# A searched instruction order, searched further from its present state: a new table for four attention layers

## The chip, the cores and the metric

The kernel runs on one core of one Trainium2 chip. The metric is device microseconds (us) of one execution; lower is better. Five engines run their own instruction streams side by side: TensorE (PE, with its weight loads shown as PEld), VectorE (DVE), ScalarE (ACT), GpSimd (POOL) and SyncE (SP, which only issues DMAs here). Each takes its instructions strictly in the order in which they were written.

## The reference

Four layers on a sequence of 2048 tokens by 512 features: A, B, A, B. Layers 1 and 3 are the same linear attention block, layers 2 and 4 the same sliding-window block.

```python
def _A_ref(x, wqkv, wo):               # linear attention, 32 heads of 16
    q, k, v = heads(x @ wqkv)
    phi = lambda t: where(t > 0, t + 1, exp(t)) + 1e-6
    pq, pk = phi(q), phi(k)
    kv = einsum("bhsd,bhse->bhde", pk, v);  z = pk.sum(over tokens)
    return merge((pq @ kv) / (pq . z + 1e-6)) @ wo

def _B_ref(x, wqkv, wo):               # softmax over a causal window of 256
    q, k, v = heads(x @ wqkv)
    p = softmax(where(0 <= i - j < 256, q @ k.T * Dh ** -0.5, -1e9))
    return merge(p @ v) @ wo

x = x + _A_ref(_layernorm(x), A_wqkv, A_wo)
x = x + _B_ref(_layernorm(x), B_wqkv, B_wo)
x = x + _A_ref(_layernorm(x), A_wqkv, A_wo)
x = x + _B_ref(_layernorm(x), B_wqkv, B_wo)
```

## The kernel before

The 2048 tokens are 16 tiles of 128 (T = 16). Everything stays in SBUF between the layers: the residual `xres`, the transposed activations or queries `XQ`, the keys `kB`, the values `vB` and three or four tiles of probabilities (`pb`, and in the last layer also the upper part of `vp`). PSUM's eight banks are each one tile of 512 float32 columns.

A class `Plan` writes the whole program as a list of 2542 small operations with their dependences; nothing is emitted yet. The operations, with the lines that the profile shows:

- The layer norm (`norm`): statistics on DVE (L382, L383), the power of -1/2 on POOL (L384), the normalised tile on DVE (L385), and its transposition by a DMA that SP issues (L391) or, for a few tiles, by PE (L397).
- Products of a tile with a weight matrix: L420 (tokens on partitions: 4 matmuls of 512 columns) and L434 (features on partitions: 16 matmuls of 128 columns). ACT or DVE copies the result out of PSUM (L409; L615 and L616 for the sliding-window keys; L404 for tiles transposed by PE).
- Linear attention: the feature map phi by an exponential on ACT (L443) and DVE or ACT steps (L444, L447, L448, L450); sums over tokens (L476, L479, L501, L524); denominators (L563), their reciprocals (L567, L568), spreading (L576) and scaling of the queries (L583).
- Sliding window: for every tile of keys, four score groups and a "far" group (L667; L709 and L712 for the far one), each into four PSUM banks; two exponentials per group on ACT (L677, L722) that read two banks each; the masks of the window's edges on DVE (L687, L736, L745) or POOL (L686, L733, L744), where either engine may do it; the values (L768, L780); the reciprocal and the division (L790, L791) on DVE; the output product (L420) and the residual (L594).
- SP issues the DMAs: loads of inputs (L291) and weights, the transpositions (L391), the rearrangement of keys and values into `kB` and `vB` (L624, L643), and most of the stores (L891; POOL issues the others).

What sets the order: a constant `TABLE` (L903 on), text that is unpacked in `place`. For every operation it holds its position in one global order, the engine that runs it (where more than one may), the PSUM bank of every tile, and which of its waits comes first. `place` adds the dependences that follow from two tiles sharing a bank, and lets a long POOL operation wait for the last wide DVE operation ahead of it. `synchronise` turns dependences into semaphore waits and leaves out those that are already implied. `Kernel.run` then lets each engine play its operations in the table's order:

```python
order = [ops[raw[2 * k] + 256 * raw[2 * k + 1]] for k in range(n)]
o.eng = ("PE", "ACT", "DVE", "POOL", "SP")[raw[2 * n + o.i]]
x.banks = [raw[3 * n + k]]
o.first = raw[3 * n + len(tiles) + o.i]
```

So one table decides who waits for whom. The score group that PE issues next needs four free banks, and those come free when ACT has read them; the other PSUM tiles come free when ACT or DVE has copied them out.

Of the kernel before, what the change touches and what calls it, by code (L numbers as in the profile page):

```python
# [231 lines left out]
class Plan:  # L232
# [675 lines left out]
    r"g^ch*omMqeSyc&Ms#I#As-h}G6&S1-PN}L84yvlQs=cbFLMQ{TR5^7^-BFp~p88S!png)Jlt48I4-w$5N(c@HsYFl&GJ}PP5E&vtJJmr2g2eDz{j7$lkSe^&",
    r"0)Zh4G*C$)v`PY5AsMuTqL3YmL3Jn&*&qj$gy5<MlvGh6In;!lPz!=UZ72bCpp+`F8mdxITNPEsR5VBdxu6WxgJ#ei+CxVu4RxUjEK|LpDYSr=&<et+Sx`sy",
    r"hUKa?Ojc7=akWCNQd3n2*r_@}7w7{K)JoM2cB$2Bx|*iCLTBg;Jz$3F2WM1w=n4JdteOMo)Iiv+_NoC;Q_Y1HP+zTt%`gx4!G5@)R>6FDqZU9twFQDgBefc4",  # L910
    r"!$MdC;nX7dMV(iRVUG$1OW?j*3+v#bs;jm_SoN!_rG8iI;R;-ZYj6PesRwEs41&S19S*`{cmjuDDLhn<)DC#8mcbC%2}9v2jD#C-7?#6zc%p8?GYAeFU>IzK",
    r"TQD3p!4U`n3IT7!E?`8w10liSQ8)>Nr(gsKeh<&#G`xV9up5G6aNGmIa4)=qd+-DNrYzot`w$YN!vpvZT48Gpg(0vFI*b8lAT&n7NEjL4sz7)QjzeJl1=?a5",
    r"j0q<o2>uFDu@L?UvEVm|4bd<rM#orK7>i&|%!M&9CFaI_SO8ODJ3I^du^0BnqL><sVF?@s8qYy)cnIgA59WbK@DmirpCKj0#)8-n^TKE-g{3hK=7aq38cJdu",
    r"EQ4|J0;GaBkQ(}9JdBSCa3EI30azBR;_r|K(qc7Ch*hvUriDZ}9MfTYtc4@7HrBwJco8l^ddz}hF)NP1u6P;3VK#gV-7qh9$MDz}2V-KagB?)QZj69KF%L2s",
    r"8Ur116pqF{I0Wm%SZn}wF$oUB9Jm+9U^yIz4WSX#!=zXNJ7H&xh~=>{Ou=MW9}nOmJc!e<3ns^@m;$HcFg$`Y@Gw@wnV11*<2LMxvv3X`!|ga0Cc;t7h?y`u",
    r"R>b4D15e;S90#j$4Q9rZI05G3c<6ywaV@UH^|%2W;3?dQr|}G)#cS9QU*S0{3+3QE{(wK?ehf<GAvkTq>v#i$Q3a?7H}MvRr4SUJ?qE22i?>nHU3Byl{)}k}",
    r"C>=Gz^z<6%;e1?xjnUFQ3{2y35(J_NI1wYzPV7jNu@g;(khB?tP-hBFTW}KQr3;vkLeW-?M$zda=BF^U3ol_YDozXWGA_c!_y%K8Oo~MrC?hq&*i?vwN>C<>",
    r"OYx{MUBNgskOt8bEJgQmFcqN(_z;_7Gb~A^sT`G|qEwceV++hdIjJS)q6$=i9$|c{PBmy4m8Y6iiykA=2pUBdX(<k;+Vl%%rYZ0QyHGtELkTD$)uH-Smqrs&",
    r"B8o_n=~qllN$4qdrQfg*jiZ7TiN;f3`W=r_7D`GD=ok&9Ni>0yQ8$W0{b(63$K#Zhrcig9Oi^hhJ;PIUhO$vZYDBZ?G>xUHG>6X73T#Z@VRmXl6R9c9rIok}",
    r"zsC!7facM8szlFmJ~gA}^a2l39(sw3XaOyz<dmB#(?U8#DX0piq)Rk}QqfuJK|QGj^`g`?fUeMGN<$%aZ<-1h=_*Z!84yZ`*4GI1b*f6!;07(BnSgpLO(W9V",  # L920
    r"=mb@xrL>Gr(h-_L+vz4vrybOvZqahuNh|0!X}yc?(0zJ9dG#!cq$BGnI;zg6TT&~^uXocPT1i240UcBa)8TY$T15{jf^I|MbwvG$+R|fsM&Hp)il(FM82Sm7",
    r")vTXVIUP$IJy6Hdv2|P>Ru9tUbxeJj2J5?&RIjE=I<ZcotLS7pxlW-g>y)~huCDh|DxF%3uA%QyO+8Uh()Dy0y^pHu$-05AufL~)`Z?{VLOQs9LA7)mZS_lf",
    r"ML$ppT~e3QwRLm-BZbgwXqv90Tj;d9u1=@Z>*>0J9;3(V8G4rfiJZ=$1L<)(qYkVa>e)J;o})AA%sPQ?seh(cy0xyThv@ivk)EkH(Gp!ox6^BBsBWVd>-Kt>",
    r"UPqg$ux_i@(-vx^H&7FON>A0Lbq9S~C(^HJxZX%_sIg9{=jo<;fnKeDr}=uRE~3xqx71P3)ob(=y-=UmN_Wz~(66*suhS#+Z*)<2)>-rgy<T6|SM(-bR2S15",
    r"^hSMEU(=g)7u{6{=G*$N4#LItNPR~K<q3L}Zl=5G(fYc+q`T`I`lvppZ|Ylmyw0k#=_mS}4#C-VC=SV6^gVrC=g>LzQ@vGh)6evFy+ePe!*Dnb%irtgIy>j!",
    r"m->Z%r6aK69$GjeN8+<OC%5Lv9GsWwHr!J$*Zs8RUV5hv#{KmQ9ff=AA9OC=mXGlXeVn850DV&T(W`V{eP8F+CpaqS(Ld_Y{FDA!hvx@62Jg}jbzI)9V{$x>",
    r"&L{b`4#Wl6aV##xr}!zK=9T)fzQoV?G8g3UI1k6?eEdf5(cg1kPQVHIIVa)5{EL3UN%;yV;v$@z6LULiPcOL`AJWM<7k8i%oS%QyMfnw1<l=l-|G;~7DgKd<",
    r"=#u<M@6)Auzy3{E;sd%1$Kivz8&~EkT$Q_W4X()@xEfdIT6~^6a&qp(DL5sk;y&Du`|<_u&KJ2er{*;LyY9hhxhKEX1DIIzK<>}&xfjpl1$>6j@_g>igLp8<",
    r"<{^BJnTN9CVVsW3aBT)I%fq=2kKnpojw^6I{*~+VNN&Il`8U4Gv-leS&eyp-&*9m8gKzR%zQxOU1>a`mJ3N=~@^W6pOIVr3ypr$nQohflcp;DGcKm=F@hTp}",
    r"Yj`!U<*~eu*K-!m${TqD|HPYk9B1RryoJZ}1pb-R^F*$1w(>U4z}`!R+0L(d2WR9ryptRAF8+m^@NUk;nZ1W(3vS8U?BT$sDF-o=crx#0Hm%s0pk^O8<6veA",  # L930
    r"H!%BoIydLw<^YSC%G3BT&)_3$jWaX(ARpz2e24>?NBo$da5fXx<TqJOPLti_GI>n_liL(Dg-kw^!xT1oOmtJkgfK--L(|BFG;K{d)7bPh#Y__u%Cs}R%uqAT",
    r"G&P}3d(+G`Hyun1)7x}3oy>64$8<K~O<xnn#4wReWYf<?FfGk&Gsny|txOlw)wDLNOdHeR3^2t_L^HyaFj35Wv)YU_3(P>X#w;{ZO-!@jEHWicDHF{cFx^Z!",
    r")7=a*gH0JT&y+Qb&02HN#4<h15mVYMHOowFGsGM<$INoG-W)fh%xJU0Y%~+hCUe4^G!xAQGs%2sCYvc{iJ5A?H|xxEbIFV`(@Y$5(Zn^U%w`i`;+fOtjJayI",
    r"nD}O_Nnl=>aVCKz6fNmxyh$X7jVG-fG8ts6S!s5e73QqjZ8AzSbJ?6X=gc*e+}t#K%oS7Kh@>#n%`LOd>@^ikO7qrOQR3vbxnn@?ntLXMyfK+1r2Jw+$pdrW",
    r"q%t$iLla15n!xhXyfQ%~v;1m)FbPd)nJ<Y<VzWT@nOP>R{APm6LJ2MrC6XjDi6x0-Fd0o`2_wNIizGFf%ytt_c9^V^*<_QQ=0_7nqDmGML$XUWi7u%mhdeSr",
    r"nbZ<fa!ML0AU~Ue(p*Sho5$vcNh;S(E_q^FNFhOKBu~xnrlk~?Jd#`5NGvHLZKbiqmb}tL+DTD~BPAuS<d=L>OiD;8DK2THw6vFwQbx*34=E=Vq`Xv=iYA$K",
    r"kV>Yf^pf6E*))~pl0rI36;oYmNL7<kx=1srX2wfRX)Rr)vviYMGC?NFaXBF;Wx33f+EPclOKMX|`pQa~EvICKERi(ky7ZA7vQ%2hB$+IyC7sNX2(nD($p)z`",
    r"b>*g<k+eo^I+NZ^5o?{DD*dFMY?M{9N!CaesVb|by166MWT4!YK~lramBF%B&dLzECz~a_43%MWPKL{R86hKOoqR8&<hi_%`qDry$$i->m!+X>kx(|Y-6;>`",
    r"iaeC<@<?_`Ap2N$%N}_m*CdP$Y_~}e`&7P@y|PaV+0k-U_R9e|D9>b!M6uEASlJ<k?R1H17t11vZj0C%@`Ie0{_>;5w72DugtZssmc+0%O?Vr@&Xl0`m0Xkr",
# [176 lines left out]
```

## Time and profile before

| | |
|---|---|
| median of 3 runs | 409.51 us (408.73 to 409.90) |
| the profiled execution | 408.54 us, of which the instructions span 406.7 us |
| busy: PE, ACT, DVE, POOL | 383.5, 355.2, 317.7, 163.7 us |
| granted TensorE clock | 0.999 |

The span is what the trace shows from the first instruction to the last; 1.8 us of the execution's time lie outside it. The span falls into six stretches that the prediction uses: 0 to 60 us the first linear layer with the loads; 60 to 210 the sliding-window layer 2, into which the first parts of layer 3 are already mixed; 210 to 260 the turn through layer 3 to layer 4; 260 to 398 layer 4; and the last tile until 406.7.

### The profile page before, as it was taken

To read this page: it belongs to the slowest core of one execution; us is meant where nothing else is said; L and a number is where in the kernel's file an instruction comes from. 1 tells how busy PE (TensorE), PEld (TensorE's weight loads), DVE (VectorE), ACT (ScalarE), POOL (GpSimd) and SP (SyncE) were. 2 spreads that over 40 slices of the span, in tenths; PEclk is the share of its full clock that TensorE was granted. 3 is DMA by queue.
4 is the path that set the end of the run, shared out by engine and by line. 5 is a ranking of instruction groups with operands and counts; after the bars stand their busy time and mean duration, and the time that the engine had idled before them with its cause. 6 is when DMAs were issued, how large, how long until landed. Compare 5 with 4: busy or idle time off the path is not lost.

```text
span 406.7 us, 18121 instructions
## 1 busy us (share of the span) xinstructions
PE 383.5 (94%) x7920; PEld 257.3 (63%) x7995; DVE 317.7 (78%) x715; ACT 355.2 (87%) x464; POOL 163.7 (40%) x261
## 2 busy tenths in 40 slices
PE   8999999999989999999999999999899999989886
PEld 4554777667556556575657767677658665756664
DVE  6985899978998898887684799986796759665455
ACT  4976999999999999999997365898999899999991
POOL 4563132424454454341545202044451346323872
PEclk9999999999999999999999999999999999999999
DMA  7777125442437524434232000434314442473451
GB/s 228 142 174 193 31 67 114 102 94 72 91 69 138 79 77 96 113 84 91 56 69 56 15 2 27 121 84 107 75 50 99 92 121 57 112 136 93 97 135 54
DMA packets 67286, 37.75 MB, mean 93 GB/s; under 512 B 47880, under 2 KB 62344, under 8 KB 67208
## 3 DMA queue, kind: packets, MB, share of 16 engines
q1 hardware_dynamic: 66816, 35.54, 38.4%
q8 instruction: 63, 1.03, 1.0%
q0 software_dynamic: 384, 1.05, 0.7%
q14 instruction: 15, 0.12, 0.1%
q10 hardware_dynamic: 8, 0.00, 0.0%
HBM read 6.29 MB, written 2.10 MB: 21 GB/s over the span
## 4 chain that ended last, share of the span: by engine, by line
PE 59%; ACT 26%; DVE 7%; issue 3%; DMA 3%; POOL 1%; SPq 1%; POOLq 0%
PE ps L420 21%; PE ps L434 15%; ACT pb L677 14%; PE ps L768 8%; PE ps L667 6%; ACT pb L722 4%; ACT vp L677 4%; PE ps L780 3%; PE ps L501 2%; ACT tE L443 1%; DVE stats L382 1%; DMA XQ<-vp 1%; PE ps L712 1%; DMA xres<-in_A_x_dram 1%; DVE xres L594 1%
## 5 line engine op out<-in xcount | busy, mean ns | idle before, releaser
L677 ACT ACTIVATE pb<-ps 128x1024 bf16<-128x1024 f32 (+3 forms) x224 | 197.9, 977 | 8.0 <-PE ps L667 7.1
L384 POOL TENSOR_TENSOR rs<-mv,negh 128x1 f32<-128x1 f32 x64 | 38.2, 596 | 89.6 <-DVE mv L383 87.2
L434 PE MATMUL ps<-xT,wBp 128*128 128x128 bf16 x1024 | 68.9, 219 | 1.3 <-DVE o L791 0.3
L434 PEld LDWEIGHTS ps<-xT,wBp 128*128 128x128 bf16 x1024 | 58.6, 98 | 12.7 <-issue 4.1
L768 PEld LDWEIGHTS ps<-vB,pb 128*128 128x128 bf16 x1712 | 54.0, 96 | 11.6 <-issue 3.6
L768 PE MATMUL ps<-vB,pb 128*128 128x52 bf16 (+1 forms) x1712 | 59.7, 184 | 0.5 <-POOL vp L744 0.2
L744 POOL TENSOR_SCALAR_AFFINE_SELECT pb<-pb 128x1024 bf16<-128x1024 bf16 x36 | 42.0, 1167 | 41.6 <-DVE xn L385 11.8
L667 PE MATMUL ps<-XQ,kB 32*128 32x256 bf16 (+2 forms) x1024 | 48.3, 262 | 3.0 <-ACT pb L677 0.9
L722 ACT ACTIVATE pb<-ps 128x1024 bf16<-128x1024 f32 x50 | 48.4, 1029 | 3.2 <-PE ps L712 2.3
L594 DVE TENSOR_TENSOR xres<-ps,xres 128x512 bf16<-128x512 f32 x63 | 43.0, 685 | 10.3 <-PE ps L420 9.8
L686 POOL TENSOR_SCALAR_AFFINE_SELECT pb<-pb 128x512 bf16<-128x512 bf16 x46 | 30.6, 666 | 46.4 <-ACT pb L677 25.0
L420 PE MATMUL ps<-wA,XQ 128*128 128x512 bf16 x176 | 46.6, 379 | 2.1 <-issue 0.6
L443 ACT ACTIVATE tE<-ps 128x512 bf16<-128x512 f32 x64 | 38.2, 609 | 10.1 <-PE ps L420 3.6
L382 DVE BATCH_NORM_STATS2 stats<-xres 128x6 f32<-128x512 bf16 x64 | 43.3, 682 | 2.7 <-DMA xres<-in_A_x_dram 2.2
L790 DVE RECIPROCAL rc<-ps 128x16 f32<-128x16 f32 x64 | 14.0, 238 | 30.3 <-PE ps L780 30.2
L434 PE MATMUL ps<-XQ,wA 128*128 128x128 bf16 x512 | 35.7, 219 | 0.0
L434 PEld LDWEIGHTS ps<-XQ,wA 128*128 128x128 bf16 x512 | 30.9, 98 | 6.8 <-issue 0.6
L667 PEld LDWEIGHTS ps<-XQ,kB 32*128 32x128 bf16 x1024 | 15.4, 92 | 29.0 <-ACT pb L677 11.3
L420 PE MATMUL ps<-wBv,xT 128*128 128x512 bf16 x102 | 28.9, 380 | 4.3 <-issue 1.8
L420 PE MATMUL ps<-wBo,oT 128*128 128x512 bf16 x108 | 29.6, 380 | 2.8 <-issue 1.4
L420 PE MATMUL ps<-M,XQ 128*128 128x512 bf16 x115 | 30.1, 380 | 1.7 <-issue 0.6
L733 POOL TENSOR_SCALAR_AFFINE_SELECT pb<-pb 128x256 bf16<-128x256 bf16 x50 | 22.2, 467 | 19.7 <-DVE pb L745 4.1
(128 smaller groups left out, 602.6 us busy)
## 6 DMA issues: line engine op xcount, KB each, us to landing
vB<-vS SPq DMA_DIRECT2D x64, 136.0 KB, 2.6
kB<-vp SPq DMA_DIRECT2D x64, 128.0 KB, 2.2
xres<-in_A_x_dram SPq DMA_DIRECT2D x6, 256.0 KB, 4.6
wA<-in_A_wqkv_dram SPq DMA_DIRECT2D x4, 256.0 KB, 3.5
pb<-in_B_wqkv_dram SPq DMA_DIRECT2D x4, 256.0 KB, 3.2
out_dram<-xres POOLq DMA_DIRECT2D x8, 128.0 KB, 3.1
out_dram<-xres SPq DMA_DIRECT2D x7, 128.0 KB, 2.4
xres<-in_A_x_dram SPq DMA_DIRECT2D x4, 128.0 KB, 2.2
```

The costliest lines, as they stand in the source:

```text
L382: self.on("DVE", "stats", lambda e: e.bn_stats(K.stats[:, t % 8, 0:6], K.xres[:, t, :]), key, dve(512), rd=[("xres", t)], wr=[("stats", t ...
L384: self.pow = self.on("POOL", "pow", lambda e: e.tensor_tensor(K.rs[:, t, :], K.mv[:, t, 1:2], K.negh[:], ALU.pow), key + 0.03, (640, 690), ...
L420: m = e.matmul(K.ps(ps), lhs(c), rhs(c), start=c == 0, stop=c == 3)
L434: m = e.matmul(K.ps(ps)[:, f * P:(f + 1) * P], w(c, f), xT(c), start=c == 0, stop=c == 3)
L443: self.on("ACT", "E", lambda e: e.activation(K.tE[:, s, :], K.ps(ps), ACT.Exp, bias=0.0), key, act(512), wr=[("tE", s)], ps=[ps])
L594: self.on("DVE", "res", lambda e: e.tensor_tensor(K.xres[:, t, :], K.ps(po), K.xres[:, t, :], ALU.add), key, dve(512), rd=[("xres", t)], w ...
L667: m = e.matmul(K.ps(two(gq // 2)[gq % 2])[:, ns * i:ns * i + ns], K.kB[rows, j % 4, 2 * f + b, :, :], K.XQ[rows, f, q:q + ns], start=True, ...
L677: return e.activation(out(h, ns).rearrange("p (f g) c -> p f g c", f=n), i, ACT.Exp, bias=0.0, scale=0.25)
L686: return e.affine_select(out=x, in_=x, compare_op=ALU.is_ge, fill=0.0, base=1, pattern=[[0, 4 * n], [2, 64]], channel_multiplier=-1)
L722: return e.activation(o.rearrange("p (f g) b c -> p f g b c", g=2), i, ACT.Exp, bias=0.0, scale=0.25)
L744: return e.affine_select(out=x, in_=x, compare_op=ALU.is_ge, fill=0.0, base=-2, pattern=[[0, 16], [-2, 64]], channel_multiplier=1)
L768: m = e.matmul(K.ps(ps[f // 2])[:, cols(f, gq, wide(f, gq))], stat(b, f, gq)[:, c:c + P], vals(b, f, gq, wide(f, gq)), start=f % 2 == 0 an ...
```

## The change

The order is searched further from its present state, with 48 draws a move and a higher first temperature. In the program that means a new `TABLE` and nothing else: the same 2542 operations, the same dependences, another global order, for some operations another of their allowed engines, and other PSUM banks. The core of the diff, one line of some sixty:

```diff
 TABLE = (
-    r"c-p;L1E3yBv+b(t>gtYd+qP}nwr$(CZQHhO+q=OcS>(;!{QF*#O?H#){%`L0&2;y4pE`A_x@PXZ5mh7=RXuj7@~dbHlv0sZ0aZ|?R%ujPRY*lwqDU21=@hFN",
...
+    r"c-qBT1HdK6(k->twr$(CZQHhO+qP}nw(VdyStPsr&+M1v1-nUhllT7lzB|*?Q&oNH)ajm?dkG>#REP%op#VH~2oWI?q=qz55DGzBC=5jaAUZs8k6a0e0S2l-",
...
 )
```

What moves, counted over the engines' streams (before to after). ACT has 463 operations before and 458 after: the weight rearrangements of L374 go from 5 to 2, the fills of L361 from 1 to 0 and of L863 from 3 to 2, the copies after a transposition (L404) from 12 to 10, the copies of L409 from 32 to 33, the key copies of L615 from 6 to 7. All 256 and 56 exponentials of L677 and L722 stay. DVE has 714 and 723: the long masks of L745 go from 16 to 22, those of L687 from 24 to 25 and of L736 from 23 to 25, L404 from 1 to 3, L409 from 62 to 61, L616 from 26 to 25. POOL has 224 and 219: the long masks of L744 go from 40 to 34, L686 from 48 to 47, L733 from 66 to 62, while L374 goes from 3 to 6, L359 from 1 to 2 and L861 from 1 to 2. PE has the same 896 operations.

PE's stream differs mostly in three regions: its first 60 us, the end of layer 2 with the turn (about 165 to 275 us), and single neighbours exchanged in between. The order of the 156 score groups is the same throughout. The PSUM banks are numbered anew almost everywhere; which operation frees a bank for which is often the same under the new numbers.

SP at the program's start (the loads of `xres` tiles and of `wA`, and the transpositions of normalised tiles into `XQ`), before:

```order
L294 DMA wA<-in_A_wqkv_dram 128x4x512
L291 DMA xres<-in_A_x_dram 128x2x512 x2
L391 DMA_TRANSPOSE XQ<-vp 128x4x128
L291 DMA xres<-in_A_x_dram 128x2x512
L391 DMA_TRANSPOSE XQ<-vp 128x4x128 x2
L291 DMA xres<-in_A_x_dram 128x2x512
L391 DMA_TRANSPOSE XQ<-vp 128x4x128
```

and now:

```order
L294 DMA wA<-in_A_wqkv_dram 128x4x512
L291 DMA xres<-in_A_x_dram 128x2x512
L391 DMA_TRANSPOSE XQ<-vp 128x4x128
L291 DMA xres<-in_A_x_dram 128x2x512 x2
L391 DMA_TRANSPOSE XQ<-vp 128x4x128
L291 DMA xres<-in_A_x_dram 128x2x512
L391 DMA_TRANSPOSE XQ<-vp 128x4x128 x3
```

The first transposition has moved ahead of one load, and two loads now stand between the first and the second. Both streams have the same loads; the first two normalised tiles that are transposed by DMA are tiles 5 and 7 before, 5 and 6 now.

ACT at the turn, from the last four score groups' exponentials of layer 2 (L722 and L677) into the feature maps of layer 3 (L443), with `oT` the transposed output of layer 2's last tile, before:

```order
L443 ACTIVATE tE<-ps 128x512
L677 ACTIVATE pb<-ps 128x4x128 x2
L677 ACTIVATE pb<-ps 128x4x64 x2
L677 ACTIVATE pb<-ps 128x4x128 x2
L404 ACTIVATE oT<-ps 128x512
L443 ACTIVATE tE<-ps 128x512 x4
L404 ACTIVATE XQ<-ps 128x4x128
L409 ACTIVATE vp<-ps 128x512
```

and now:

```order
L443 ACTIVATE tE<-ps 128x512
L677 ACTIVATE pb<-ps 128x4x128 x2
L677 ACTIVATE pb<-ps 128x4x64 x2
L677 ACTIVATE pb<-ps 128x4x128 x2
L863 ACTIVATE vp<-zc 128x1152
L443 ACTIVATE tE<-ps 128x512
L409 ACTIVATE vp<-ps 128x512
L443 ACTIVATE tE<-ps 128x512 x7
```

The copies of `oT` and of one transposed tile of `XQ` have left ACT for DVE, and a fill of `vp` has come from POOL and stands where the copy of `oT` stood.

ACT in layer 4, around tiles 5 to 7 of the keys (about 300 to 323 us), with L615 the copy of new keys and L409 that of queries or values, before:

```order
L722 ACTIVATE pb<-ps 128x8x2x64 x2
L677 ACTIVATE pb<-ps 128x4x224 x6
L722 ACTIVATE pb<-ps 128x8x2x64 x2
L677 ACTIVATE pb<-ps 128x4x224 x10
L409 ACTIVATE XQ<-ps 128x4x128
L722 ACTIVATE pb<-ps 128x8x2x64 x2
```

and now:

```order
L722 ACTIVATE pb<-ps 128x8x2x64 x2
L677 ACTIVATE pb<-ps 128x4x224 x6
L722 ACTIVATE pb<-ps 128x8x2x64 x2
L615 ACTIVATE vp<-ps 128x512
L677 ACTIVATE pb<-ps 128x4x224 x8
L409 ACTIVATE XQ<-ps 128x4x128
L677 ACTIVATE pb<-ps 128x4x224 x2
L722 ACTIVATE pb<-ps 128x8x2x64 x2
```

One copy of keys has come from DVE to ACT and stands between the exponentials; the copy of queries has moved two exponentials forward.

More of the change, by code (lines that the diff above doesn't have):

```diff
@@ L908 @@
[L908 to L939, printed above, removed]
@@ L960 @@
+    r"{E+NVD~~O&y7WQs9~5SMA$oz?Pu8ah{k;#wXTpO696*cDpZ{LqPZ?h+LIJ^jqX04a=U_ZWe3+h{rv+abp4>gYKIqs>)zhPY)r06^LecOg8~#Zjetr~$e}n@6",
+    r"3G9Eg;h*>5M=U<-^4|o8Uzk3AK`HSc*YMXz{G9UPZy|ro{}09aXukL<@4uVQ&q(kK1cbi@L;r$oKfu9%VPgLiDgIKKe_iQcG7<hlh+jNU@E<Q9|BWT-zdPRl",
+    r"PnLgCieCzX|1{E{CV(Hmhv8>3f}ckt{x9jrFVPkLyG6y%%?-a`7T{kyehJn11@}h$IQ#ggqx|MeoKI@^{{YyWG8z",
 )
```

75 lines of the change are left out of this document (52 added, 23 removed).

## The prediction

> **What bounds the kernel now.** I read the page's busy times first, then the busy times of the six stretches, then who waits for whom on PE, and last the timeline at single waits. The page's first part says how full the engines are:
>
> ```profile
> span 406.7 us, 18121 instructions
> PE 383.5 (94%) x7920; PEld 257.3 (63%) x7995; DVE 317.7 (78%) x715; ACT 355.2 (87%) x464; POOL 163.7 (40%) x261
> ```
>
> PE is idle for 406.7 - 383.5 = 23.2 us in all, and no order of the same instructions can take more than that from it. The busy times by stretch (after the times: length, then PE, PEld, DVE, ACT, POOL) show where:
>
> ```profile
> 7.00:60.00 53.00, 52.12 (x556) 32.69 (x563) 44.30 (x119) 44.17 (x78) 22.38 (x42) 1.00 0.56 136
> 60.00:90.00 30.00, 29.40 (x513) 20.01 (x518) 25.72 (x59) 28.77 (x35) 9.52 (x14) 1.00 0.48 101
> 90.00:210.00 120.00, 114.07 (x2469) 73.68 (x2491) 101.35 (x220) 116.50 (x134) 52.32 (x67) 1.00 0.40 86
> 210.00:260.00 50.00, 48.37 (x827) 34.92 (x834) 40.01 (x89) 31.23 (x54) 12.13 (x17) 1.00 0.16 37
> 260.00:330.00 70.00, 66.84 (x1693) 48.16 (x1704) 53.34 (x113) 65.43 (x82) 28.74 (x51) 1.00 0.38 90
> 330.00:398.00 68.00, 62.02 (x1768) 42.20 (x1776) 44.18 (x98) 66.55 (x84) 33.75 (x56) 1.00 0.46 105
> ```
>
> Two kinds of stretch alternate. From 7 to 60 and from 210 to 260 us PE is the bound: it idles 0.9 and 1.6 us there, and ACT has 8.8 and 18.8 us to spare. From 90 to 210 and from 330 to 398 ACT is: it idles 3.5 and 1.5 us, and PE waits for it. From 60 to 90 and 260 to 330 both are nearly full (ACT idles 1.2 and 4.6 us, PE 0.6 and 3.2). So the room for a better order is what the bounding engine idles in each stretch: 0.9 + 1.2 + 3.5 + 1.6 + 4.6 + 1.5 = 13.3 us, 3.3% of the time; the rest of PE's idle time is the price of ACT's work. Some of PE's idle time is no order's business either: from the list of waits on PE,
>
> ```profile
> PE ps L420 <- issue: 4.5, 28, 0.2
> PE ps L1029 <- DVE kB L1021: 1.3, 1, 1.3
> PE ps L420 <- ACT pb L677: 1.2, 2, 0.7
> PE ps L420 <- DVE rc L790: 1.1, 3, 0.5
> PE ps L667 <- ACT pb L677: 0.9, 3, 0.5
> PE ps L420 <- DMA XQ<-vp: 0.2, 1, 0.2
> ```
>
> 4.5 us in 28 pieces have no releaser ("issue"), 1.3 us are the start. The others are many and short. What they look like, PE at two places of layers 2 and 4:
>
> ```profile
> 113.14 0.40 PE L667 MATMUL ps<-XQ,kB 32*128 32x256 bf16 x8
> 114.27 0.81 PE L420 MATMUL ps<-wBv,xT 128*128 128x512 bf16 x3 [0.73 <-ACT pb L677]
> 115.52 0.40 PE L667 MATMUL ps<-XQ,kB 32*128 32x256 bf16 x8 [0.44 <-DVE o L791]
> ...
> 372.73 0.62 PE L434 MATMUL ps<-xT,wBp 128*128 128x128 bf16 x8 [0.32 <-DVE o L791]
> 373.66 0.71 PE L712 MATMUL ps<-XQ,kB 32*64 32x64 bf16 x64 [0.31 <-ACT pb L677]
> ```
>
> Each is a PSUM bank that ACT or DVE has not yet emptied.
>
> **The change part by part.** PE's work, the exponentials and the order of the 156 score groups stay. I went through the 39 places where PE lost most (the step from one operation's end to the next against the quick quarter of the same pairs) and asked which operation frees the bank or brings the data there in the new table. At 35 of them it is the same operation as before, under another bank number, among them the waits at 114.27, 115.52 and 373.66 above; at 372.73 the bank now comes from an exponential. Those waits I cost at nothing: they stay. That leaves five edits.
>
> The start. PE waits there for one transposition by DMA:
>
> ```profile
> 17.75 1.90 PE L420 MATMUL ps<-wA,XQ 128*128 128x512 bf16 x8 [0.24 <-DMA XQ<-vp]
> ```
>
> The new order issues the first transposition ahead of a load, transposes tile 6 second, and asks for tile 7 later on PE, so these 0.24 us can go; the loads that now stand behind the transpositions bring the tiles from 10 on, which PE's stream takes well after tile 7. The stretch holds 0.9 us in all. Bounds: a gain of 0.9, a loss of as much if a load comes late. I take a gain of 0.2. What is late next is PE itself, which is then gap-free up to 60 us.
>
> ACT in the first 60 us loses three weight rearrangements and two fills:
>
> ```profile
> L374 ACT ACTIVATE wBp<-pb 128x512 bf16<-128x512 bf16 x5 | 3.7, 767 | 0.0
> L863 ACT ACTIVATE vp<-zc 128x1152 bf16<-128x1152 bf16 x3 | 3.5, 1154 | 0.0
> ```
>
> 3 x 0.77 + 2 x 1.15 (the second kind of fill priced like the first) = 4.6 us. Hidden by PE, the bound there: nothing gained. POOL takes them, ahead of the norms' powers of layer 2; it is busy 22.4 of 53 us, so nothing is lost either.
>
> The end of layer 2 and the turn. Two copies of values (L409) between 200 and 216 us go from ACT to DVE, and `oT` leaves ACT, which stood behind it for long:
>
> ```profile
> L409 ACT ACTIVATE vp<-ps 128x512 bf16<-128x512 f32 x6 | 3.4, 601 | 0.6 <-PE ps L420 0.6
> 221.11 0.66 ACT L677 ACTIVATE pb<-ps 128x256 bf16<-128x256 f32 x2 [0.79 <-PE ps L667]
> 228.16 0.60 ACT L404 ACTIVATE oT<-ps 128x512 bf16<-128x512 bf16 x1 [4.69 <-PE ps L397]
> ```
>
> The copies are worth at most 2 x 0.6 = 1.2 us, if ACT is the bound where they stood; after 208 us it waits for PE, so I take 0.4. The 4.69 us are ACT's, while PE is busy 48.4 of 50 us: at most 1.6 us, of which I take 0.3. Below nothing: DVE gets these copies, but it is busy 40.0 of 50 us, and I allow 0.5 us of loss.
>
> Layer 4. ACT gets one copy of keys and one of queries from DVE and gives up one small copy of reciprocals:
>
> ```profile
> L615 ACT ACTIVATE vp<-ps x6: 747/751/786, 54.4 to 253.8; 128x512 bf16<-128x512 f32 x6
> L409 ACT ACTIVATE XQ<-ps 128x512 bf16<-128x512 f32 x10 | 6.0, 604 | 1.0 <-PE ps L434 0.8
> L568 ACT ACTIVATE rec<-recf x3: 302/310/311, 45.0 to 290.7; 128x128 bf16<-128x128 f32 x3
> 312.63 3.35 ACT L677 ACTIVATE pb<-ps 128x896 bf16<-128x896 f32 x4 [0.76 <-PE ps L667]
> ```
>
> 0.75 + 0.60 - 0.31 = 1.04 us more for the engine that ends this layer. The copy of keys stands just ahead of the exponentials that end in the wait of 0.76 us, which may swallow it whole. Bounds: 0 and 1.04 us lost; I take 0.4. From 330 us on ACT's stream is full (66.55 of 68 us) and both streams hold the same exponentials in the same order to the end but for the last pair, so nothing can be won back there.
>
> The masks. DVE gets nine more (six long ones), POOL eleven fewer:
>
> ```profile
> L745 DVE TENSOR_TENSOR pb<-pb,tri 128x1024 bf16<-128x1024 bf16 x14 | 10.6, 758 | 0.0
> L687 DVE TENSOR_TENSOR pb<-pb,tri 128x512 bf16<-128x512 bf16 x22 | 9.9, 450 | 2.5 <-ACT pb L677 2.2
> ```
>
> 6 x 0.76 + 3 x 0.45 = 5.9 us more for DVE, spread over layers 2 and 4, where it idles 120 - 101.4 = 18.6 and 138 - 97.5 = 40.5 us. Cost at nothing, with that idle time as the cover; if it is gone at a place, see the second rival.
>
> The sum: -0.2 - 0.4 - 0.3 + 0.4 = -0.5 us, against the profiled execution's 408.54 us (span 406.7 us and 1.8 us around it): 408.0 us. Its median of three runs is 409.51 us, 1.0 us above that execution, and the new kernel will be judged by a median too: 409.51 - 0.5 = 409.0 us.
>
> **The rivals.** First: many small gains. The table moves hundreds of operations by a place or two, and I priced only the moves that I could name. Of the 13.3 us of room, a fifth would be 2.7 us: 409.5 - 2.7 = 406.8 us. For it speaks that neighbours are exchanged everywhere and single waits lie between 0.2 and 0.8 us; against it that the longest waits keep their causes. The point from which it decides is the start of ACT's full stretch, at 330 us: what is gained before must show as an earlier start there.
>
> Second, slower: masks that collide. A DVE instruction now and then takes far longer while POOL works; DVE first, then POOL at the same times:
>
> ```profile
> 108.83 1.41 DVE L745 TENSOR_TENSOR pb<-pb,tri 128x1024 bf16<-128x1024 bf16 x1
> 112.18 1.33 DVE L385 TENSOR_SCALAR xn<-xres,mv,rs 128x512 bf16<-128x512 bf16 x1
> ...
> 108.56 1.14 POOL L744 TENSOR_SCALAR_AFFINE_SELECT pb<-pb 128x1024 bf16<-128x1024 bf16 x1 [0.65 <-ACT pb L722]
> 112.22 1.15 POOL L744 TENSOR_SCALAR_AFFINE_SELECT pb<-pb 128x1024 bf16<-128x1024 bf16 x1 [1.18 <-ACT pb L722]
> ...
> L745 DVE TENSOR_TENSOR pb<-pb,tri x14: 673/682/1406, 89.2 to 394.9; 128x1024 bf16<-128x1024 bf16 x14
> ```
>
> 1.41 against a median of 0.68 us: a collision costs DVE 0.7 us. If three more such masks stand ahead of a division (L791) on which PE waits, the time is 409.5 + 3 x 0.7 = 411.6 us. Below about 0.7 us of slack in front of those divisions it decides. Against it: DVE has idle time, and the number of instructions that can collide grows little. The Trainium skill (SBUF — State Buffer, section on SBUF's two separate sides) has the rule behind it: DVE and GpSimd share a port pair as an exclusive lock, and whoever comes second is blocked for the other's whole instruction, a DVE operation with two SBUF inputs included. By that rule the change, which gives DVE six more long masks of that kind, can only add collisions; the trace agrees on the mechanism, with the 1.41 us above.
>
> Third, the case that the new table is no other order for the chip, only other numbers, is in my forecast: no change that a measurement can tell.
>
> **How the numbers follow.** About 0.3% (1.2 us) is what a measurement of this kernel can tell from no change. No change that can be told: 0.46, with 408.3 to 410.7 us and 409.0 as its likeliest value. The first rival, faster: 0.37, because three of the four named terms point down and the room on that side, 13.3 us, is far larger than what they take of it. The second, slower: 0.17. For the range I keep the gains' far ends, 0.9 + 1.2 + 1.6 = 3.7 us, 405.8 us, and the losses' ends, of which the collisions are the largest, 2.1 us, nearly 411.6; of each I leave out the outermost tenth: 405.8 to 411.2 us.
>
> **What would show it.** Right: PE's waits at about 114 and 373 us are there again with the same releasers, ACT is 66 to 67 us busy in its last 68 us, and the last stretch starts within 1 us of 330. The start: no wait for a transposition before 20 us. The turn: ACT's 4.69 us in front of `oT` gone, PE as full as before. Layer 4: the wait of 0.76 us at 312 filled by the copy of keys. Wrong: PE's idle time below 21 or above 25 us, or long masks on DVE with a mean well above 0.76 us and PE waiting for divisions.

## The result, and the profile after

| | before | changed |
|---|---|---|
| median of the runs taken side by side | 409.83 us (408.73 to 411.19) | 407.62 us (407.22 to 408.41) |
| the profiled execution | 408.54 us, span 406.7 | 407.40 us, span 405.6 |

The ratio is 0.9947, with a 95% interval of 0.9927 to 0.9967: faster by 0.5%, 1.3 to 3.0 us. Run again on another chip it was 407.73 us against 408.99, ratio 0.9970 (0.9959 to 0.9981). The time lies in the range of the prediction, but the case that came is its first rival (many small gains), not the forecast (no change that can be told).

The page's first part, changed kernel:

```profile
span 405.6 us, 18107 instructions
PE 382.8 (94%) x7922; PEld 257.7 (64%) x7995; DVE 321.6 (79%) x724; ACT 350.8 (86%) x459; POOL 155.4 (38%) x254
```

The same line of a second execution of the changed kernel (span 405.8 us):

```profile
PE 392.1 (97%) x7995; PEld 257.8 (64%) x7995; DVE 322.0 (79%) x724; ACT 350.8 (86%) x459; POOL 156.3 (39%) x254
```

PE's busy time differs by 9.3 us between two executions of one program, because 73 matmul records are missing in the first: there are as many matmuls as weight loads, 7995. Before's profile shows 7920 of them. The 4.5 us of pauses without a releaser ("issue"), which the prediction read as PE's own, are these missing records: the second execution's list of waits has none at L420. PE's idle time, 23.2 us before and 22.8 after, therefore tells nothing; with all records it is 405.8 - 392.1 = 13.7 us.

By stretch, changed kernel (times, length, then PE, PEld, DVE, ACT, POOL):

```profile
7.00:60.00 53.00, 52.07 (x557) 32.69 (x564) 45.15 (x120) 38.92 (x73) 26.32 (x46) 1.00 0.53 135
210.00:260.00 50.00, 48.46 (x887) 35.77 (x896) 43.79 (x96) 31.18 (x53) 8.32 (x13) 1.00 0.19 40
260.00:330.00 70.00, 67.24 (x1724) 48.52 (x1734) 54.16 (x118) 66.83 (x83) 25.00 (x46) 1.00 0.37 88
330.00:398.00 68.00, 61.84 (x1691) 42.08 (x1704) 44.55 (x102) 65.50 (x83) 29.21 (x50) 1.00 0.45 104
```

ACT is fuller from 260 to 330 us (66.83 against 65.43) and has less left after 330 (65.50 against 66.55): its work is done earlier.

The busy times don't show where a microsecond went. What does: both orders have the same 156 score groups in the same order, so the end of one and the same group can be compared between two traces. Where the programs are alike, two traces keep their distance to 0.02 us over a hundred microseconds; where they differ, it jumps (it also jumps at two places where they are alike, about 312 and 379 us, to which the text comes back). The distance to before's trace at eight groups, in us (below zero is ahead; the head row gives the time in before's trace):

| trace | 69.7 | 111.7 | 120.2 | 204.0 | 260.9 | 294.1 | 331.4 | 397.1 |
|---|---|---|---|---|---|---|---|---|
| changed | +0.29 | -0.28 | -0.78 | -0.75 | -1.00 | -1.16 | -1.45 | -0.90 |
| changed, second | +0.66 | +0.12 | -0.38 | -0.36 | -0.59 | -0.60 | -1.53 | -1.25 |

Before 70 us the distance also holds the chance of each execution's first loads: their first product (L420) begins 0.45 and 0.28 us earlier than in before's trace. From there on three steps stand out: 0.50 us between 111.7 and 120.2, about 0.25 between 204 and 261, 0.3 to 0.9 between 294 and 331. The rest goes down and up: the 0.5 us that both traces gain between 69.7 and 72 us, for one, are lost as 0.62 between 66.7 and 69.7.

### The profile page after: what moved, and what is told of

Same layout as the page of the kernel before. It is cut to its first block, busy times and chain, and to the rows that moved or that the text cites. A ratio compares the mean times of both kernels' runs of the same rounds, so it can differ in the third digit from the quotient of the medians.

```text
span 405.6 us, 18107 instructions
## 1 busy us (share of the span) xinstructions
PE 382.8 (94%) x7922; PEld 257.7 (64%) x7995; DVE 321.6 (79%) x724; ACT 350.8 (86%) x459; POOL 155.4 (38%) x254
## 4 chain that ended last, share of the span: by engine, by line
PE 64%; ACT 29%; DVE 3%; issue 2%; DMA 1%; SPq 0%; POOL 0%
PE ps L420 22%; ACT pb L677 18%; PE ps L434 16%; PE ps L768 7%; ACT pb L722 6%; PE ps L667 5%; PE ps L501 3%; ACT vp L677 3%; PE ps L780 3%; PE ps L712 1%; PE ps L1029 1%; ACT tE L443 1%; PE ps L709 1%; DMA kB<-vp 1%; ACT vp L722 1%
## 5 line engine op out<-in xcount | busy, mean ns | idle before, releaser
L677 ACT ACTIVATE pb<-ps 128x1024 bf16<-128x1024 f32 (+3 forms) x224 | 197.9, 980 | 7.4 <-PE ps L667 6.1
L384 POOL TENSOR_TENSOR rs<-mv,negh 128x1 f32<-128x1 f32 x64 | 36.3, 567 | 93.7 <-DVE mv L383 92.0
L443 ACT ACTIVATE tE<-ps 128x512 bf16<-128x512 f32 x64 | 38.4, 612 | 16.3 <-PE ps L434 5.5
L686 POOL TENSOR_SCALAR_AFFINE_SELECT pb<-pb 128x512 bf16<-128x512 bf16 x45 | 30.0, 667 | 56.8 <-ACT pb L677 38.8
L722 ACT ACTIVATE pb<-ps 128x1024 bf16<-128x1024 f32 x50 | 48.5, 1032 | 3.4 <-PE ps L712 2.0
L420 PE MATMUL ps<-wA,XQ 128*128 128x512 bf16 x176 | 45.1, 379 | 2.0 <-issue 1.1
L744 POOL TENSOR_SCALAR_AFFINE_SELECT pb<-pb 128x1024 bf16<-128x1024 bf16 x32 | 37.2, 1164 | 22.2 <-DVE tE L444 7.1
L733 POOL TENSOR_SCALAR_AFFINE_SELECT pb<-pb 128x256 bf16<-128x256 bf16 x52 | 22.5, 457 | 41.8 <-ACT pb L677 30.5
L420 PE MATMUL ps<-wBv,xT 128*128 128x512 bf16 x104 | 29.0, 380 | 4.5 <-ACT pb L677 1.7
L420 PE MATMUL ps<-wBo,oT 128*128 128x512 bf16 x109 | 29.8, 380 | 2.6 <-issue 1.0
L420 PE MATMUL ps<-M,XQ 128*128 128x512 bf16 x114 | 30.2, 380 | 1.9 <-issue 0.6
```

The lines of the kernel that those rows point to most:

```text
L384: self.pow = self.on("POOL", "pow", lambda e: e.tensor_tensor(K.rs[:, t, :], K.mv[:, t, 1:2], K.negh[:], ALU.pow), key + 0.03, (640, 690), ...
L420: m = e.matmul(K.ps(ps), lhs(c), rhs(c), start=c == 0, stop=c == 3)
L443: self.on("ACT", "E", lambda e: e.activation(K.tE[:, s, :], K.ps(ps), ACT.Exp, bias=0.0), key, act(512), wr=[("tE", s)], ps=[ps])
L677: return e.activation(out(h, ns).rearrange("p (f g) c -> p f g c", f=n), i, ACT.Exp, bias=0.0, scale=0.25)
L686: return e.affine_select(out=x, in_=x, compare_op=ALU.is_ge, fill=0.0, base=1, pattern=[[0, 4 * n], [2, 64]], channel_multiplier=-1)
L722: return e.activation(o.rearrange("p (f g) b c -> p f g b c", g=2), i, ACT.Exp, bias=0.0, scale=0.25)
```

## The step at 115 us

The prediction showed two waits of PE, at 114.27 and 115.52 us, and held that both stay since the same operations free the banks. PE in the changed kernel at that place (and, last, at the two places of layer 4 that the prediction showed):

```profile
112.86 0.40 PE L667 MATMUL ps<-XQ,kB 32*128 32x256 bf16 x8
114.00 0.81 PE L420 MATMUL ps<-wBv,xT 128*128 128x512 bf16 x3 [0.73 <-ACT pb L677]
114.74 0.40 PE L667 MATMUL ps<-XQ,kB 32*128 32x256 bf16 x8
...
371.44 0.62 PE L434 MATMUL ps<-xT,wBp 128*128 128x128 bf16 x8 [0.44 <-ACT pb L677]
372.25 0.74 PE L712 MATMUL ps<-XQ,kB 32*64 32x64 bf16 x64 [0.19 <-DVE vp L736]
```

The first wait is there to the hundredth (0.73 us in both; in traces with all matmul records it is 0.51, since one of this row's four matmuls is missing here). The second (0.44 us for DVE's division, L791) is gone, though the same division frees the bank: it comes earlier. DVE in before's trace and then, changed, DVE and POOL:

```profile
114.26 0.33 DVE L790 RECIPROCAL rc<-ps 128x16 f32<-128x16 f32 x2
114.62 0.76 DVE L791 TENSOR_TENSOR o<-ps,rc 128x256 bf16<-128x256 f32 x2
115.29 1.11 DVE L385 TENSOR_SCALAR xn<-xres,mv,rs 128x512 bf16<-128x512 bf16 x1
```

```profile
111.31 0.68 DVE L745 TENSOR_TENSOR pb<-pb,tri 128x1024 bf16<-128x1024 bf16 x1
112.97 0.37 DVE L790 RECIPROCAL rc<-ps 128x16 f32<-128x16 f32 x2 [0.99 <-PE ps L780]
113.38 0.76 DVE L791 TENSOR_TENSOR o<-ps,rc 128x256 bf16<-128x256 f32 x2
114.05 0.51 DVE L385 TENSOR_SCALAR xn<-xres,mv,rs 128x512 bf16<-128x512 bf16 x1
...
112.06 2.36 POOL L744 TENSOR_SCALAR_AFFINE_SELECT pb<-pb 128x1024 bf16<-128x1024 bf16 x2 [0.59 <-DVE pb L745]
```

In front of before's division stood the two DVE instructions that the prediction quoted as collisions with POOL: a mask of 1.41 us (median 0.68) and a normalisation of 1.33 us. Now the mask runs while POOL waits for it (0.59 us), the normalisation stands behind the division, and DVE even idles 0.99 us ahead of the reciprocals. The division ends 1.2 us earlier, 1.0 of it beyond the 0.28 us by which this trace is ahead anyway. So the mechanism of the second rival was at work, with the opposite sign: the new order takes collisions away from in front of this division.

## The experiments

Every kernel below has the same operations as before; only the table differs. "Cut" means: one order up to a point, the other behind it, with the banks of the second assigned anew where they clash. Cut times are before's. Ratios are to before, timed side by side.

**The parts alone.** The changed kernel again, and its three regions one at a time:

```diff
  changed kernel                                    (e0)
- order, engines, banks up to 60 us: before
+ order, engines, banks up to 60 us: new            (e1: the rest is before's)
- 60 to 257 us: before
+ 60 to 257 us: new                                 (e2: the rest is before's)
- 257 us to the end: before
+ 257 us to the end: new                            (e3: the rest is before's)
```

Expected, in this order:

> The changed kernel unaltered, timed on the same chip as the three that follow. Both theories: about 2.2 us below the kernel before (ratio 0.995, between 0.993 and 0.997). If the gain is partly one of steadiness, its runs lie within 1.2 us of each other and those of the kernel before within 2 us or more.

> The new order up to the first score group of layer 2 (about 60 us), the old one from there on. Theory 'many small pieces from 60 us on': PE is gap-free in the first 60 us in either order, so 0 to 0.3 us below the kernel before (ratio 0.999 to 1.000). Rival 'the start': the first stretch holds the gain, 1.5 to 2.2 us below (ratio 0.995 to 0.996).

> The old order up to the first score group of layer 2, the new one from there to the first score group of layer 4 (about 257 us), the old one again for layer 4. Theory 'many small pieces': the two traces differ by 1.1 us between those two points, so 1.0 to 1.5 us below the kernel before (ratio 0.9965 to 0.9975). Rivals 'the start' and 'layer 4': 0 to 0.3 us.

> The old order up to the first score group of layer 4, the new one for layer 4. Theory 'many small pieces': the two traces differ by less than 0.4 us over this layer, which ACT bounds, and ACT has 1.0 us more work in it: between 0.4 us below and 0.5 us above the kernel before (ratio 0.999 to 1.001). Rival 'layer 4': 1.5 us or more below.

| | median, us | ratio | distance at 69.7 | 204.0 | 260.9 | 397.1 |
|---|---|---|---|---|---|---|
| changed again | 407.73 | 0.9970 (0.9959 to 0.9981) | +0.66 | -0.36 | -0.59 | -1.25 |
| start alone | 409.68 | 1.0021 (1.0008 to 1.0035) | +1.69 | +1.67 | +1.84 | +1.86 |
| layer 2 and turn | 410.42 | 1.0029 (1.0016 to 1.0043) | +1.51 | +0.53 | +1.59 | +1.98 |
| layer 4 alone | 409.17 | 1.0003 (0.9992 to 1.0014) | +0.39 | +0.37 | +1.48 | +0.78 |

None of the theories of a single part holds: by the medians the parts lose 0.7, 1.4 and 0.2 us where the whole gains 1.3 (only the third lies where "many small pieces" put it). Nor is the new order steadier: 408.09 to 409.85 us before and 406.72 to 408.42 changed, about the same width. The table shows why the parts lose: at the cuts. The second loses 0.7 us between 60 and 72 us and 1.3 between 221 and 261, the third 1.1 between 221 and 261, at waits that neither whole order has. PE at about 258 us, second and then third kernel:

```profile
257.90 0.37 PE L667 MATMUL ps<-XQ,kB 32*128 32x224 bf16 x8 [0.84 <-DVE XQ L583]
```

```profile
259.38 0.60 PE L420 MATMUL ps<-M,XQ 128*128 128x512 bf16 x2 [0.82 <-DVE vp L616]
```

The first loses most of its time before its cut, where it is the changed kernel's order: a transposition landed late for PE in its profiled execution.

```profile
33.86 1.04 PE L420 MATMUL ps<-wA,XQ 128*128 128x512 bf16 x4 [1.12 <-DMA XQ<-vp]
```

Inside its stretch each keeps the gains: 0.50 us at 115 in the second, 0.6 between 294 and 331 in the third. The next cuts therefore lie where the two orders have done nearly the same operations.

**One operation moved.** If the step at 115 us is a collision's, one normalisation put behind the division in before's order brings it:

```diff
  (DVE, before's table, about 112 us)
  L383 BN_AGGR mv<-stats 128x2
- L385 TENSOR_SCALAR xn<-xres,mv,rs 128x512
  L382 BN_STATS stats<-xres 128x6
  L383 BN_AGGR mv<-stats 128x2
  L790 RECIPROCAL rc<-ps 128x16 x2
  L791 TENSOR_TENSOR o<-ps,rc 128x8x2x16 x2
+ L385 TENSOR_SCALAR xn<-xres,mv,rs 128x512
  L385 TENSOR_SCALAR xn<-xres,mv,rs 128x512
```

> The kernel before with one operation moved: the normalised tile (L385) that DVE writes at 112.18 us, stretched to 1.33 us beside a POOL mask, stands behind the division (L791) of 114.62 instead of ahead of it. Theory of collisions ahead of a division: the division ends 1.0 to 1.3 us earlier, PE's wait of 0.44 us at 115.52 is gone, and from there on everything comes 0.4 to 0.5 us earlier to the end: 408.99 - 0.45 = 408.5 us on this chip, ratio 0.999. Rival, that the wait belongs to the bank's order and not to DVE's delay: the wait stays and the ratio is 1.000. Rival, that a gain in layer 2 is taken back by a later wait: it shows at 120 us and is gone at 398.

Measured: 408.62 us against 409.65, ratio 0.9972 (0.9962 to 0.9982). DVE and then PE in its trace:

```profile
113.63 0.37 DVE L790 RECIPROCAL rc<-ps 128x16 f32<-128x16 f32 x2
114.04 0.75 DVE L791 TENSOR_TENSOR o<-ps,rc 128x256 bf16<-128x256 f32 x2
114.71 0.72 DVE L385 TENSOR_SCALAR xn<-xres,mv,rs 128x512 bf16<-128x512 bf16 x2
...
114.66 0.81 PE L420 MATMUL ps<-wBv,xT 128*128 128x512 bf16 x3 [0.73 <-ACT pb L677]
115.40 0.40 PE L667 MATMUL ps<-XQ,kB 32*128 32x256 bf16 x8
```

The two normalisations together take 0.72 us where they took 1.33 + 1.11, PE's second wait is gone, and the distance goes from +0.38 to -0.12 between 111.7 and 120.2: a step of 0.50 us, as in the changed kernel. Layer 2 takes back 0.1 of it (-0.02 at 204). The trace itself ends 0.64 us behind before's, since it loses 1.0 us behind 331 us, 0.7 of them at the pause that the last section shows. So it is the medians that show the gain at the end, and they say more than the step, 0.7 to 1.6 us; what the rest is stays open.

The run moves the instruction and does not separate its place from its length. A normalisation with no long POOL instruction beside it takes about 0.4 us (0.40 in before's trace at 106.77), so its place alone would bring at most 0.4 of the 1.0 us by which the division comes earlier here, and the rest is the collision's. That is argued from these durations. The Trainium skill (SBUF — State Buffer, section on SBUF's two separate sides) says that DVE and GpSimd hold a shared port pair as an exclusive lock, the loser blocked for a whole instruction. The 2.44 against 0.72 us of the same two instructions agrees; who came first the trace does not show for the first of them, whose record begins 0.04 us ahead of POOL's (112.18 and 112.22) and which is stretched all the same.

**The stretch from 290 to 335 us, a kept start, and ACT's copies.**

```diff
- 290 to 335 us: before                              
+ 290 to 335 us: new                                 (e5: the rest is before's)
- up to 103 us: new
+ up to 103 us: before                               (e6: the rest is the changed kernel's)
- engines in layer 4: key copy DVE, query copy DVE, reciprocal copy ACT
+ engines in layer 4: key copy ACT, query copy ACT, reciprocal copy DVE   (e7: order and banks before's)
```

> The kernel before with the new order only between 290 and 335 us (PE operations 650 to 736), cut at both ends where the two orders have done all but one or two of the same operations. Theory of separate local gains: PE ends this stretch 0.8 to 1.1 us earlier and keeps it: 408.0 to 408.2 us, ratio 0.998. The prediction's term for this stretch (ACT's copies): 0.4 us lost, ratio 1.001. Rival of one fabric, that a piece of the new order pays only with the rest: a loss of 0.7 to 1.5 us at a cut, as at the three cuts of the first experiments, ratio 1.001 to 1.003.

> The changed kernel with the order of before up to 103 us (232 PE operations), cut where the two orders have done all but one of the same operations. Theory of separate local gains: the new start is worth 0.2 to 0.4 us less than nothing (counted from PE's first operations to 71 us), so this kernel is 0.3 us faster than the changed one: 407.4 us on the chip of the first experiments, ratio 0.996. The prediction's term for the start: 0.2 us slower than the changed one, ratio 0.9975. Rival of one fabric: a loss of about 1 us at the cut, ratio 0.999 or above.

> The kernel before, in its own order and banks, with three operations of layer 4 on the engines of the new table: one copy of keys and one of queries from DVE to ACT, one small copy of reciprocals from ACT to DVE. The prediction's term: 0.4 us lost (0 to 1.04), 409.4 us, ratio 1.001. Theory that these copies fill pauses of ACT: within 0.2 us of before up to 330 us, ratio 1.000. Rival, that ACT's full last stretch pays for each: the start of the last stretch moves by 0.7 to 1.0 us, ratio 1.002.

| | median, us (before: 409.65) | ratio | distance at 69.7 | 111.7 | 294.1 | 331.4 | 397.1 |
|---|---|---|---|---|---|---|---|
| 290 to 335 us | 408.46 | 0.9965 (0.9953 to 0.9977) | -0.05 | -0.05 | -0.10 | -1.11 | -0.54 |
| start kept | 408.60 | 0.9972 (0.9957 to 0.9988) | +0.19 | +1.11 | +0.30 | -0.60 | -0.71 |
| ACT's copies | 410.62 | 1.0021 (1.0007 to 1.0035) | +0.91 | +0.91 | +1.77 | +1.62 | +2.34 |

The stretch alone gains 1.0 us on before's trace, of which 0.2 to 0.3 are chance: other traces with before's order there, such as that of the moved normalisation (from -0.04 to -0.37), gain 0.18 to 0.33 on it as well. About 0.7 us are the new order's. Where from, ACT shows; before's trace, after the wait of 0.76 us that the prediction quoted, and then the changed kernel's:

```profile
316.62 3.35 ACT L677 ACTIVATE pb<-ps 128x896 bf16<-128x896 f32 x4 [0.64 <-PE ps L667]
319.82 0.63 ACT L409 ACTIVATE XQ<-ps 128x512 bf16<-128x512 f32 x1
320.98 1.94 ACT L722 ACTIVATE pb<-ps 128x1024 bf16<-128x1024 f32 x2 [0.53 <-PE ps L712]
...
324.71 3.54 ACT L677 ACTIVATE pb<-ps 128x896 bf16<-128x896 f32 x4 [0.17 <-PE ps L667]
```

```profile
308.78 0.75 ACT L615 ACTIVATE vp<-ps 128x512 bf16<-128x512 f32 x1
309.36 5.18 ACT L677 ACTIVATE pb<-ps 128x896 bf16<-128x896 f32 x6
315.54 1.73 ACT L677 ACTIVATE pb<-ps 128x896 bf16<-128x896 f32 x2 [0.99 <-PE ps L667]
317.15 0.60 ACT L409 ACTIVATE XQ<-ps 128x512 bf16<-128x512 f32 x1
...
319.94 1.94 ACT L722 ACTIVATE pb<-ps 128x1024 bf16<-128x1024 f32 x2 [0.47 <-PE ps L712]
321.76 5.04 ACT L677 ACTIVATE pb<-ps 128x896 bf16<-128x896 f32 x6
```

ACT waited 0.76 + 0.64 + 0.53 + 0.17 = 2.1 us for PE there; now it waits 0.99 + 0.47 = 1.46 us, and has one copy more to do. Over the same exponentials ACT waits 1.65 to 1.93 us in the traces of the start alone, of layer 2 with the turn and of the moved normalisation, which have before's order there, and 0.93 to 1.13 us in four others with the new order (changed again, layer 4 alone, this stretch, start kept). Which of the moved operations does it was not separated.

The copies on ACT without the new order cost 0.8 us, and all of it is the query copy's, between 261 and 294 us. On ACT it stands behind two exponentials and a feature map and runs at 276.90 instead of DVE's 274.13, and PE's next score group waits for its bank (the row names a DVE copy that ends in the same 0.1 us). ACT and PE in that kernel:

```profile
276.90 0.59 ACT L409 ACTIVATE XQ<-ps 128x512 bf16<-128x512 f32 x1
...
277.63 0.37 PE L667 MATMUL ps<-XQ,kB 32*128 32x224 bf16 x8 [0.83 <-DVE vS L409]
```

The key copy and the reciprocals, between 294 and 331 us, cost little (the distance falls by 0.15 there, in other traces of before's order by 0.18 to 0.33). So the engine alone is a loss of 0.8 us, which the new order takes in by what stands around it. It is as much as the rival of a full last stretch had expected (0.7 to 1.0 us), but it comes from PE's wait at 277 us.

The kept start tells nothing on the start: at its cut PE waits 1.13 us for an exponential, where both whole orders wait 0.20 us. Behind it, the distance falls by 1.8 us to the end, through the same steps as in the changed kernel.

**Two places together, then three.**

```diff
- L385 ahead of the division at 114.6 us; 290 us to the end: before
+ L385 behind it; 290 us to the end: new                                  (e8)
+ and 200 to 255 us: new                                                  (e9)
```

> The kernel before with the one normalisation moved (as in the run that moved it alone) and the new order from 290 us (PE operation 645) to the end, cut where all PSUM banks follow each other alike in both. Theory of separate local gains: 0.45 us at 115 us, 0.4 to 0.8 us between 305 and 330, both kept: ratio 0.996 to 0.9975, as the changed kernel itself (0.9959 and below). Rival of one fabric: no better than either part alone, ratio 0.998 or above.

> The same, with the new order between about 200 and 255 us as well (PE operations 459 to 591); the start to 200 us is that of before but for the one normalisation. Theory of separate local gains: another 0.4 us, gained at 211 to 215 us, ratio 0.995 to 0.9965, and as fast as the changed kernel or up to 0.3 us faster, since the start of before is kept. Rival of one fabric: a loss of 0.7 to 1.2 us where this stretch is cut in, ratio 0.998 or above.

The first: 407.89 us against 409.02, ratio 0.9967 (0.9954 to 0.9980), as the changed kernel itself on the other chip. The 0.50 us at 115 and 0.9 between 294 and 331 are both in its trace. The second: 412.29 us, ratio 1.0089 (1.0074 to 1.0104); it loses 4.4 us between 204 and 221 at its cut, where PE waits for an exponential and for a division, and then runs slowly:

```profile
207.90 0.97 PE L768 MATMUL ps<-vB,pb 128*128 128x52 bf16 x32 [1.62 <-ACT pb L677]
...
210.92 0.56 PE L667 MATMUL ps<-XQ,kB 32*128 32x256 bf16 x8 [1.44 <-DVE o L791]
211.41 1.89 PE L420 MATMUL ps<-wA,XQ 128*128 128x512 bf16 x4
```

The same four matmuls take 1.04 us in the kernel with layer 2 and the turn alone. The busy times by stretch show why (the third figure from the right is the granted clock):

```profile
205.00:211.00 6.00, 2.94 (x95) 2.30 (x97) 4.03 (x10) 2.84 (x5) 2.27 (x2) 1.00 0.36 34
211.00:214.40 3.40, 3.40 (x22) 0.90 (x22) 0.69 (x1) 1.94 (x2) 0.81 (x2) 0.50 0.46 98
214.40:220.00 5.60, 5.60 (x105) 3.31 (x99) 3.61 (x7) 5.04 (x8) 1.25 (x3) 1.00 0.08 16
```

Behind 6 us in which PE was busy for 2.94, the clock granted to it was half for 3.4 us. From 211.41 to the next score group's end PE took 3.16 us, against 1.74 for the same operations in the kernel with layer 2 and the turn alone: 1.4 of the 4.4 us are the clock's. All five executions of this kernel have a mean granted clock of 0.991 to 0.995 (the changed kernel's 0.999 to 1.000).

What the end of layer 2 and the turn are worth by themselves could thus not be told beyond the 0.26 us that the kernel with layer 2 and the turn alone gains between 204 and 221. None of these kernels is faster than the changed one.

**Engines alone.** Before's order and banks, with the masks, and then the start's fills and rearrangements, on the engines of the new table:

```diff
- 81 masks (L686/L687, L733/L736, L744/L745) on before's engine
+ each on the new table's engine                                         (e10)
- four L374, two L861/L863, one L359/L361 in the first 60 us: ACT; one L374: POOL
+ the same seven: POOL; the one L374: ACT                                (e11)
```

> The kernel before, in its own order and banks, with all 81 masks that run on another engine in the new table on that engine; DVE gets nine more of them in sum. The prediction's term: nothing, ratio 1.000, with long masks on DVE (L745) at a mean of 0.76 us or less. Second rival (collisions ahead of divisions): three or more longer DVE masks, 411 us, ratio 1.005. Theory of a table that is matched to its order: masks on the wrong engine for the order around them stand in line and PE waits, 1 to 4 us, ratio 1.003 to 1.010, with PE's waits for DVE grown and not its waits for ACT.

> The kernel before, in its own order and banks, with the weight rearrangements (four to POOL, one to ACT), one constant's rearrangement and two fills of the first 60 us on the engines of the new table: 4 to 5 us less work on ACT there. The prediction's term: nothing, because PE bounds this stretch: the same time within 0.2 us, ratio 1.000, with ACT busy 39 to 40 us between 7 and 60 us (44.2 before). Rival, that ACT holds PE there: 0.3 to 0.9 us gained, ratio 0.998 to 0.999. Rival, that POOL delays the norms of layer 2: PE waits between 60 and 90 us, ratio 1.001 to 1.003.

The masks: 415.63 us, ratio 1.0162 (1.0147 to 1.0177), the largest effect of all, and more than the 1 to 4 us expected. Long masks on DVE are not slower (mean 0.765 us, 0.758 before), so these are not collisions. PE's waits of over 0.15 us for DVE sum to 9.5 us and those for ACT to 3.6; in the next kernel's trace, which has the same PE stream and all matmul records too, they are 3.9 and 4.1. So 5.6 of the 6.6 us are waits for DVE. One of the places, DVE and then PE:

```profile
177.69 0.42 DVE L791 TENSOR_TENSOR o<-ps,rc 128x256 bf16<-128x256 f32 x1
179.60 0.43 DVE L687 TENSOR_TENSOR pb<-pb,tri 128x512 bf16<-128x512 bf16 x1 [1.48 <-ACT pb L677]
179.94 0.42 DVE L791 TENSOR_TENSOR o<-ps,rc 128x256 bf16<-128x256 f32 x1
...
180.41 0.40 PE L667 MATMUL ps<-XQ,kB 32*128 32x256 bf16 x8 [1.41 <-DVE o L791]
```

A mask that came from POOL stands between two divisions and waits 1.48 us for its exponential; the second division waits behind it, and PE for that. How much of the loss comes instead from the kernel's rule that a long POOL operation waits for the last wide DVE operation ahead of it was not separated.

The start without ACT's work: 410.08 us against 409.02, ratio 1.0023 (1.0011 to 1.0036), with ACT busy 38.24 us between 7 and 60 us where it was 44.17. Less work for ACT gained nothing, and POOL's added fill moved its other work onto DVE's. DVE, POOL, ACT and PE:

```profile
26.23 1.02 DVE L448 TENSOR_TENSOR XQ<-XQ,tE 128x512 bf16<-128x512 bf16 x1
...
26.16 0.85 POOL L346 TENSOR_SCALAR_AFFINE_SELECT spread<-spread 128x512 bf16<-128x512 bf16 x1
...
27.29 0.60 ACT L443 ACTIVATE tE<-ps 128x512 bf16<-128x512 f32 x1 [0.73 <-DVE XQ L448]
...
29.16 0.61 PE L501 MATMUL ps<-vp 128*128 128x512 bf16 x2 [0.41 <-DVE vp L448]
```

The DVE instruction takes 1.02 us beside POOL's (its like take 0.42), ACT waits 0.73 us for it, and further along the same chain PE waits 0.41. PE loses 1.1 us in three steps at about 30, 45 and 55 us, after 0.3 us gained at the wait for the transposition at 18 us; between 60 and 90 us, where one rival looked for the loss, it loses nothing.

## Why the prediction was right or wrong

**The waits that stay, priced at nothing: the step that failed first.** The releaser of a bank is the same operation at 35 of 39 places, but an operation that is the same can come earlier, because something else stands ahead of it. At 114.27 us the price was right (0.73 us again); at 115.52 it was wrong by 0.50 us, shown by moving one operation. Of the two others shown, the one at 372 us is for an exponential now (0.44 us), as said, and the one at 373.66 is 0.19 us for a mask.

**Layer 4: the wrong sign.** The price was +0.4 us, with bounds of 0 and 1.04. Between 294 and 331 us the seven traces with the new order there gain 0.3 to 1.0 us on before's (mean 0.8), five with before's order 0.15 to 0.33 (mean 0.25), which is chance; so some 0.5 us are gained. That the key copy fits into ACT's pause was right (no wait of 0.76 us ahead of those exponentials any more). What was missed: ACT's pauses of 2.1 us in that stretch were room for a better order, and the bounds left out a gain. "The last stretch starts within 1 us of 330" failed: with all steps up to there it starts 1.45 and 1.53 us earlier, the point that the first rival had named as its own, and ACT is 65.50 us busy in its last 68, not 66 to 67.

**The end of layer 2 and the turn: a third of the size.** Priced at -0.4 - 0.3 = -0.7 us; between 204 and 261 us the changed traces gain 0.25 and 0.23. ACT's 4.69 us in front of `oT` are gone, as said, and a wait of 3.02 us at the next feature map has come instead; PE is as full as before, and fuller than the prediction could see: with all matmul records it is 49.57 of 50 us busy there in before's order (start alone) and 49.79 in the new one, so that 0.4 us, not 1.6, were the bound.

**The start: gained and given back.** The transposition's wait of 0.24 us is gone, and PE is further ahead at 23 us than at 10, by some 0.2 to 0.6 us (an estimate from the weight loads begun by then). At 44.72 us it waits 0.39 us for reciprocals that it did not wait for before. At 111.7 us the two traces are -0.28 and +0.12: nothing, where -0.2 was forecast.

**ACT's relief at nothing, masks at nothing: right as sums, wrong as reasons.** ACT has 38.9 us of work where it had 44.2, and PE no less to do. But "nothing is lost either" is not so by itself: with the engines alone, moving these operations costs 0.7 us in the trace and 1.1 by the medians. The masks the same: with the new order DVE's long masks take 0.71 us in the mean (0.76 before), while their engines alone cost 1.6%. DVE's idle time was no cover: at the place shown, what counts is what stands behind the mask in DVE's queue.

**The second rival's mechanism** was right and its sign wrong: a collision decided a wait of PE. DVE instructions that take over 0.2 us more than their median number 13 in before's trace and 12 and 13 in the changed ones, but in an unbroken run of at most 4 us ahead of a division they are three before and one now.

**The size, and luck.** The steps sum to 0.5 + 0.25 + 0.5 = 1.25 us, where the prediction's sum was 0.5. That the sum has the right sign is luck: it came from a start that gained nothing, a turn priced at almost three times its size and a layer 4 with the wrong sign, and it left out the step of 0.5 us at 115. The range held because it was laid out for the first rival too. By its own rule (the outermost tenth left out at both ends) it would have been 406.2 to 411.4 us; the low end that was written, 405.8, is the untrimmed one. The two intervals hold 0.8 to 1.7 and 1.3 to 3.0 us; the profiles differ by 1.1. A part of the medians' surplus may lie behind 331 us: six other traces with before's order there lose 0.3 to 1.0 us more than before's own (mean 0.55), six with the new order -0.1 to 0.55 (mean 0.10). Before's profiled execution, at 408.54 us, was one of its quicker ones. That is argued from few traces and not shown.

## What to carry to other kernels

When the same operations run in another order, compare the end of the same operation in both traces: a gain of 0.5 us in 400 stands out as a step, and one operation moved at that place shows its cause. A wait that keeps its releaser need not keep its length; ask what stands ahead of the releaser in its own queue, and whether any of it runs beside POOL. An operation's engine and its place in the queue are one choice: the new masks' engines in the old order cost 1.6%. Pieces of an order paid only where both orders had done nearly the same work at the cut, and not at every such cut: the kept start lost 0.9 us at its own. And compare the number of matmul records with that of the weight loads before reading PE's idle time.
